# Attention scores of the first batch element as plain float32 products, 64 rows deep, in a three-layer kernel

## The chip, the cores and the metric

The kernel runs on one core of one Trainium2 chip. The metric is the time of one execution on the device in microseconds (us), as the median of several runs. A profile of one execution comes with it: each engine's instructions with start, length and what they waited for. The engines are TensorE (PE in the profile, its weight loads are PEld), VectorE (DVE), ScalarE (ACT), GpSimd (POOL) and SyncE (SP, which here issues all transfers).

## What is computed

Three layers follow one another: an attention that is causal by blocks of 64 positions, and two mixtures. Only the scores of the attention change here.

```python
B, H, S, D = 4, 8, 576, 64
scores = scale * np.matmul(q, k.transpose(0, 1, 3, 2))       # scale = 1/8
scores = np.where(block_i >= block_j, scores, -1e9)          # blocks of 64 positions
scores = scores - np.max(scores, axis=-1, keepdims=True)
attn = np.exp(scores)
attn = attn / (np.sum(attn, axis=-1, keepdims=True) + 1e-09)
x = np.matmul(attn, v)                                       # -> (2304, 512)
h = np.maximum(np.maximum(x @ w1, x @ w2), x @ w3) @ w_out   # first mixture, 512 -> 768 -> 512
# second mixture: 4 experts, each max(h @ w1[e], 0) @ w2[e], weighted by domain_probs
```

Everything is float32 in and out.

## The kernel before

**Pairs of heads.** The 8 heads of a batch element are worked on as 4 pairs; `g < NPAIR` in `load_pair` and `prep_pair` means a pair of batch element 0 (called batch 0 below), and in `scores`, `turn_probs` and `values` the number `g` counts heads, so that `g < H` means batch 0. Batch 0 takes its products of probabilities and values in plain float32 (`values32`, L310 to L322); the later batches split them in two parts.

**Scores by a split.** TensorE multiplies the type `F32R` with one pass and less precision than float32. So the kernel splits each operand in a rounded high part and the remainder. The host lays q and k out so that the 64 rows of a head stand twice, one below the other (128 rows). `keys` rounds both copies on ScalarE (L85; VectorE for pair 0) and replaces the lower one by the remainder (L122, VectorE): `kk` holds the high part in rows 0 to 63 and the low part in rows 64 to 127. `queries` makes `q1` (scaled by -1/8 and rounded, ScalarE, L133) and `q2` (the remainder, VectorE, L135). One product of `q1` with `kk` and one of `q2` with `kk`, each 128 rows deep, add up to the full score (L190). Pairs 0 and 2 (and later even ones) have their results in tiles `q1`, `q2`, `kk`, pairs 1 and 3 in `spare`, a tile that the first mixture needs only later.

**Blocks of queries.** A head has four blocks of 128 queries (`i` 0 to 3, against 128, 256, 384 and 512 keys), and the last 64 queries of both heads of a pair share one block of 128 (`i == 4`, 576 keys): zero columns beside the tails of `q1` and `q2` keep the heads apart, which takes four products. After each block but the last, `corner` (128 rows, bf16, 64 columns, L195) pushes the masked corner out of the way. VectorE takes the minimum of each block (L208), ScalarE the exponential with its sum (L215), VectorE the reciprocal of the sum (L223, L224), GpSimd the division (L226), TensorE turns the result over (L264), VectorE and ScalarE copy it to `eh` (L273, L289), and TensorE multiplies with the values.

**Order.** The program is written head by head, with the scores two heads ahead of the values; a scheduler moves instructions within each engine's list when the kernel is built. Beside the attention of batch 0 runs the conversion of the first mixture's weights (`Convert`, L418 to L453), which are handed over in float64 and turned into float32 by integer work on ScalarE, VectorE and GpSimd, while two heads of batch 1 are already begun. When all four pairs of batch 0 are through, the first mixture's products start (L505) and run between the attention of the later batches. The second mixture (L858, L940, L1017) follows.

## Time and profile before

| | |
|---|---|
| median of 3 runs | 1253.38 us (1252.73 to 1253.74) |
| the profiled execution | 1249.91 us, its span 1248.1 us |
| TensorE busy over the span | 1211.2 us (97%), 7417 products |
| VectorE, ScalarE, GpSimd busy | 929.7, 517.8, 357.1 us |
| mean granted TensorE clock | 0.996 |

The profiled execution's own time stands 1.8 us above its span (from the first to the last instruction), and 3.5 us below the median. A page of the profile gives busy time per engine, the span in slices, the chain of work that ended last, and groups of instructions; the trace behind it can be asked for any stretch, line or engine. Matmuls overlap in the records, so that the start of one and the start of the next tell its price better than its own length.

### The profile page before, as it was taken

What the parts mean: (1) busy time and instruction counts of PE and PEld (TensorE: products, weight loads), DVE (VectorE), ACT (ScalarE), POOL (GpSimd) and SP (SyncE); (2) the same over time, 40 slices, a digit from 0 to 9 for tenths busy, and PEclk for the clock granted to TensorE, in tenths of its full rate; (3) what the DMA queues carried; (4) which work ended last, traced back from release to release, by engine and by line L of the source; (5) the groups of instructions that cost most, each with busy time, mean ns of one, the idle gap of its engine ahead of it and who ended that gap; (6) DMA issues with size and microseconds to landing.
All of it is one profiled execution on the core that took longest, in us unless ns stands there. A gap on an engine that the chain in (4) does not pass through costs nothing.

```text
span 1248.1 us, 19730 instructions
## 1 busy us (share of the span) xinstructions
PE 1211.2 (97%) x7417; PEld 1157.8 (93%) x7417; DVE 929.7 (74%) x1716; ACT 517.8 (41%) x1076; POOL 357.1 (29%) x444
## 2 busy tenths in 40 slices
PE   7879998999999999999999999999999999999998
PEld 5669997999999999989999998999999999999998
DVE  7978988666565634377888896758787888686896
ACT  7977767544544421233444441233232223322222
POOL 3957786454344212243333341000000000000000
PEclk9999999999999999999999999999999999999999
DMA  8745574554533488478887864778888887776754
GB/s 304 248 164 197 170 265 161 172 153 155 183 102 119 120 287 304 150 303 332 312 311 296 310 247 162 287 274 316 300 306 311 315 314 281 253 258 228 253 210 170
DMA packets 82644, 299.69 MB, mean 240 GB/s; under 512 B 8748, under 2 KB 18036, under 8 KB 69492
## 3 DMA queue, kind: packets, MB, share of 16 engines
q1 hardware_dynamic: 82548, 298.42, 67.3%
q8 instruction: 59, 0.97, 0.3%
q14 instruction: 37, 0.30, 0.1%
HBM read 215.26 MB, written 83.14 MB: 239 GB/s over the span
## 4 chain that ended last, share of the span: by engine, by line
PE 74%; DVE 10%; DMA 5%; POOL 4%; ACT 3%; issue 3%; SPq 0%; DVEq 0%; ACTq 0%; POOLq 0%
PE m L858 24%; PE m L505 19%; PE o L1017 17%; PE st L190 3%; PE pv L359 2%; PE o L940 2%; PE o L943 2%; PE o L944 2%; DMA t<-in_e_w 2%; PE m L1017 2%; POOL p L226 2%; PE tt L264 2%; DVE mn L208 2%; DMA part<-in_e_w 1%; POOL arena L443 1%
## 5 line engine op out<-in xcount | busy, mean ns | idle before, releaser
L505 PE MATMUL m<-xh,wt 128*128 128x288 f32 x1120 | 238.4, 298 | 0.7 <-ACT mt L541 0.4
L858 PE MATMUL m<-t,w 128*128 128x384 f32 x1152 | 228.5, 336 | 0.0
L1017 PE MATMUL o<-hx,w 128*128 128x384 f32 x1176 | 225.7, 337 | 0.0
L1017 PEld LDWEIGHTS o<-hx,w 128*128 128x128 f32 x1176 | 207.8, 188 | 0.1
L858 PEld LDWEIGHTS m<-t,w 128*128 128x128 f32 x1152 | 203.4, 188 | 2.5 <-DVE tmp L878 0.4
L505 PEld LDWEIGHTS m<-xh,wt 128*128 128x128 f32 x1120 | 183.7, 188 | 1.6 <-DVE mt L543 0.8
L858 PE MATMUL m<-b,w 128*128 128x384 f32 x864 | 175.7, 337 | 2.0 <-ACT tmp L883 2.0
L505 PE MATMUL m<-xl,wt 128*128 128x288 f32 x560 | 165.3, 295 | 0.0
L858 PEld LDWEIGHTS m<-b,w 128*128 128x128 f32 x864 | 153.2, 188 | 5.1 <-ACT tmp L883 2.3
L226 POOL TENSOR_SCALAR p<-p,sm 128x128 f32<-128x128 f32 (+1 forms) x144 | 98.7, 702 | 52.1 <-DVE sm L223 17.0
L505 PEld LDWEIGHTS m<-xl,wt 128*128 128x128 f32 x560 | 105.3, 188 | 0.3
L878 DVE TENSOR_TENSOR tmp<-m,tmp 128x384 f32<-128x384 f32 x144 | 77.9, 550 | 19.4 <-PE m L858 19.2
L505 PE MATMUL m<-hh,wo 128*128 128x288 f32 x384 | 81.3, 299 | 2.9 <-ACT arena L554 1.3
L215 ACT ACTIVATE p<-st,mn 128x128 f32<-128x128 f32 (+3 forms) x144 | 78.5, 555 | 8.2 <-DVE mn L208 6.3
L988 ACT CAST hx<-hq 128x768 fp32r<-128x768 f32 x49 | 40.6, 837 | 99.0 <-PE o L1017 75.9
L190 PE MATMUL st<-kk,q 128*128 128x128 f32 (+4 forms) x336 | 71.2, 340 | 8.7 <-ACT q L133 5.5
L940 PE MATMUL o<-w,hh 128*128 128x512 f32 x192 | 74.7, 391 | 0.9 <-ACT hh L918 0.6
L813 POOL TENSOR_TENSOR w<-part,w 128x512 fp32r<-128x512 f32 x32 | 49.2, 1557 | 91.3 <-ACT w L811 61.2
L943 PE MATMUL o<-w,hh 128*128 128x512 f32 x192 | 74.7, 390 | 0.0
L944 PE MATMUL o<-w,hl 128*128 128x512 f32 x192 | 74.1, 390 | 0.0
L543 DVE TENSOR_TENSOR mt<-m,mt 128x288 f32<-128x288 f32 x96 | 43.2, 452 | 40.3 <-PE m L505 39.9
L264 PE MATMUL tt<-ident,p 128*128 128x128 f32 x400 | 61.0, 278 | 9.8 <-POOL p L226 5.4
(169 smaller groups left out, 2173.8 us busy)
## 6 DMA issues: line engine op xcount, KB each, us to landing
w<-kb SPq DMA_DIRECT2D x55, 1024.0 KB, 6.1
w<-ka SPq DMA_DIRECT2D x30, 1792.0 KB, 7.9
ka<-w SPq DMA_DIRECT2D x16, 1792.0 KB, 6.7
wt<-held SPq DMA_DIRECT2D x54, 512.0 KB, 4.1
kb<-part SPq DMA_DIRECT2D x16, 1024.0 KB, 7.0
kb<-w SPq DMA_DIRECT2D x16, 768.0 KB, 4.7
arena<-in_w SPq DMA_DIRECT2D x18, 512.0 KB, 4.0
wo<-held SPq DMA_DIRECT2D x12, 768.0 KB, 4.5
```

Source lines behind the costliest of these rows:

```text
L190: nc.tensor.matmul(out=st[:, o + c:o + c + n], lhsT=pair[part][:, q0:q0 + P], rhs=pair["kk"][:, x, c:c + n], start=m == 0, stop=m == len(t ...
L215: nc.scalar.activation(x, st[:, o:o + w], ACTF.Exp, bias=mn[:, col:col + 1], scale=-1.0, accum_out=sm[:, col:col + 1],)
L226: nc.gpsimd.tensor_scalar(x, x, sm[:, col:col + 1], 1.0, op0=ALU.mult, op1=ALU.mult)
L264: nc.tensor.transpose(tt[:, c:c + P], pt[i][:, k0:k0 + P], ident)
L505: nc.tensor.matmul(out=out_, lhsT=w, rhs=x, start=m == 0, stop=m == n - 1)
L813: eng.tensor_tensor(w[:, a:b, 1], raw[:, a:b], f(w[:, a:b, 0]), op=ALU.subtract)
L858: ins = nc.tensor.matmul(out=m, lhsT=a, rhs=b, start=start and n == 0, stop=stop and n == 3 * KH - 1, skip_group_check=True,)
L878: nc.vector.tensor_tensor(t, x, y, op=ALU.add)
L940: ins = nc.tensor.matmul(out=o, lhsT=hh[:, ts], rhs=wh, start=i == 0, stop=False)
L943: nc.tensor.matmul(out=o, lhsT=hh[:, ts], rhs=wl, start=False, stop=False)
L944: nc.tensor.matmul(out=o, lhsT=hl[:, ts], rhs=wh, start=False, stop=i == G - 1)
L1017: nc.tensor.matmul(out=o, lhsT=a, rhs=b, start=start and m == 0, stop=stop and m == 2, skip_group_check=True,)
```

## The change

For pairs of batch 0 nothing is split. The host adds an input `qk` in which a pair's k and q stand once, head 0 in rows 0 to 63 and head 1 in rows 64 to 127; a pair takes one transfer of 576 KB (pair 0: two of 288 KB) where it took two of 576 KB (pair 0: four of 288 KB). The four pairs land in two tiles that the first mixture takes later (`hh`, `hl`; the name is `plain`), so all four loads can be issued at once. The preparation is three instructions: q's first 512 queries are scaled by -1/8 in place, and the last 64 queries of the two heads are scaled into the corners of `last`, a block of 128 by 128 whose other two corners were set to zero. VectorE does that for pair 0, GpSimd for pairs 1 to 3. A block's score is then one product in float32 (type F32) over the 64 rows of its head, and the shared last block one product over all 128 rows, block-diagonal. `last` has two places, so pairs 2 and 3 write where pairs 0 and 1 were read. Later batches keep the split.

```diff
@@ -89,14 +89,23 @@
     def load_pair(g):
         b, h0 = divmod(2 * g, H)
 
-        if g % 2:
-            raw = ap_.tile([P, 2, 2, S], F32, name="raw", tag="raw")[:]
+        if g < NPAIR:
+            if g == 0:
+                pairs["hh"] = mp.tile([P, 3, 2, S], F32, name="plain", tag="hh")
+                pairs["hl"] = mp.tile([P, NF, S], F32, name="plain", tag="hl")
+                for n in range(2):
+                    nc.gpsimd.memset(pairs["hl"][:, 2 + n, 0:P].bitcast(U32), 0)
+            raw = pairs["hh"][:, g] if g < 3 else pairs["hl"][:, 0:2]
+            for n in ((0, 1), (1, 2)) if g == 0 else ((0, 2),):
+                nc.sync.dma_start(out=raw[:, n[0]:n[1]], in_=qk[g, :, n[0]:n[1]])
         else:
-            o = (B - 1) * KD * S
-            raw = arena[:, o:o + 4 * S].rearrange("p (n h s) -> p n h s", n=2, h=2)
-        for hs in ((0, 1), (1, 2)) if g == 0 else ((0, 2),):
+            if g % 2:
+                raw = ap_.tile([P, 2, 2, S], F32, name="raw", tag="raw")[:]
+            else:
+                o = (B - 1) * KD * S
+                raw = arena[:, o:o + 4 * S].rearrange("p (n h s) -> p n h s", n=2, h=2)
             for n, src in ((1, k), (0, q)):
-                nc.sync.dma_start(out=raw[:, n, hs[0]:hs[1]], in_=src[b, h0 // 2, :, hs[0]:hs[1]])
+                nc.sync.dma_start(out=raw[:, n], in_=src[b, h0 // 2])
 
         vraw = ap_.tile([P, 5, 2, D], F32, name="vraw", tag="vraw", bufs=4)
         nc.sync.dma_start(out=vraw, in_=v[b, h0 // 2])
@@ -106,19 +115,25 @@
 
 
         raw, vraw = pairs[g]["raw"], pairs[g]["vraw"]
-        if g < NPAIR and g % 2:
-
-            spare = mp.tile([P, 2 * QW + 2 * S], F32R, name="spare", tag="hh")
-            q1, q2 = spare[:, 0:QW], spare[:, QW:2 * QW]
-            kk = spare[:, 2 * QW:].rearrange("x (h s) -> x h s", h=2)
-        else:
-            q1, q2 = (ap_.tile([P, QW], F32R, name=x, tag=x, bufs=1)[:] for x in ("q1", "q2"))
-            kk = ap_.tile([P, 2, S], F32R, name="kk", tag="kk", bufs=1)[:]
+        if g < NPAIR:
+            engine = nc.gpsimd if g else nc.vector
+            last = pairs["hl"][:, 2 + g % 2, 0:P]
+            x = raw[:, 1]
+            engine.tensor_scalar(x[:, 0:S - 64], x[:, 0:S - 64], -scale, 0.0, op0=ALU.mult, op1=ALU.add)
+            for half, at in ((lo, 0), (hi, 64)):
+                engine.tensor_scalar(
+                    last[half, at:at + 64], x[half, S - 64:S], -scale, 0.0, op0=ALU.mult, op1=ALU.add
+                )
+            pairs[g].update(k=raw[:, 0], q=x, last=last)
+            yield
+            return
+        q1, q2 = (ap_.tile([P, QW], F32R, name=x, tag=x, bufs=1)[:] for x in ("q1", "q2"))
+        kk = ap_.tile([P, 2, S], F32R, name="kk", tag="kk", bufs=1)[:]
         for x in (q1, q2):
             nc.gpsimd.memset(x[:, QT + 64:QT + 128].bitcast(U32), 0)
 
         def keys(hs):
-            (rounded if g else lambda _, to, x: rounded(nc.vector, to, x))(nc.scalar, kk[:, hs], raw[:, 1, hs])
+            rounded(nc.scalar, kk[:, hs], raw[:, 1, hs])
             nc.vector.tensor_tensor(kk[hi, hs], raw[hi, 1, hs], f(kk[hi, hs]), op=ALU.subtract)
 
         def queries(hs):
@@ -134,18 +149,10 @@
             for high, low, src in zip(*parts, srcs):
                 nc.vector.scalar_tensor_tensor(low, src, -scale, f(high), op0=ALU.mult, op1=ALU.subtract)
 
-        if g == 0:
-            for h in range(2):
-                keys(slice(h, h + 1))
-                queries(slice(h, h + 1))
-            yield
-        else:
-            keys(slice(0, 2))
-            yield
-            queries(slice(0, 2))
+        keys(slice(0, 2))
+        yield
+        queries(slice(0, 2))
         pairs[g].update(q1=q1, q2=q2, kk=kk)
-        if g < NPAIR:
-            return
         vs = ap_.tile([P, 2, 5, P], F32R, name="vs", tag="vs", bufs=2)
         vh = vs[:, :, :, 0:64]
         src = vraw.rearrange("p j h d -> p h j d")
@@ -177,19 +184,25 @@
             sets.append((st, plan))
             for i, o, w in plan:
 
-                if i == 4:
-                    todo = [(QT + 64 * x, x) for x in range(2)]
+                if g < H:
+                    own = both if i == 4 else hi if h else lo
+                    terms = [(pair["last"] if i == 4 else pair["q"][own, P * i:P * i + P], pair["k"][own])]
+                elif i == 4:
+                    terms = [
+                        (pair[part][:, QT + 64 * x:QT + 64 * x + P], pair["kk"][:, x])
+                        for x in range(2) for part in ("q1", "q2")
+                    ]
                 else:
-                    todo = [(h * QT // 2 + P * i, h)]
+                    q0 = h * QT // 2 + P * i
+                    terms = [(pair[part][:, q0:q0 + P], pair["kk"][:, h]) for part in ("q1", "q2")]
                 c = 0
                 while c < w:
                     n = min(w - c, 512 - (o + c) % 512)
-                    terms = [(part, q0, x) for q0, x in todo for part in ("q1", "q2")]
                     ends = masked and i < 4 and c + n == w
-                    for m, (part, q0, x) in enumerate(terms):
+                    for m, (qs, ks) in enumerate(terms):
                         nc.tensor.matmul(
-                            out=st[:, o + c:o + c + n], lhsT=pair[part][:, q0:q0 + P],
-                            rhs=pair["kk"][:, x, c:c + n], start=m == 0, stop=m == len(terms) - 1 and not ends,
+                            out=st[:, o + c:o + c + n], lhsT=qs, rhs=ks[:, c:c + n],
+                            start=m == 0, stop=m == len(terms) - 1 and not ends,
                         )
                     if ends:
                         nc.tensor.matmul(
@@ -1301,6 +1314,8 @@
     for name in ("q", "k"):
         x = inputs[name].reshape(B, H // 2, 2, S, D).transpose(0, 1, 4, 2, 3)
         laid[name] = np.concatenate((x, x), axis=2)
+    x = np.stack([inputs[name][0].reshape(H // 2, 2, S, D) for name in ("k", "q")])
+    laid["qk"] = x.transpose(1, 2, 4, 0, 3).reshape(H // 2, P, 2, S)
     x = np.zeros((B, H // 2, 5 * P, 2, D), np.float32)
     x[:, :, 0:512] = inputs["v"][:, :, 0:512].reshape(B, H // 2, 2, 512, D).transpose(0, 1, 3, 2, 4)
     x[:, :, 5 * P - (S - 512):] = inputs["v"][:, :, 512:].reshape(B, H // 2, 2, S - 512, D).transpose(0, 1, 3, 2, 4)
```

Lines behind the scores have new numbers: L190 is L203, L195 is L208, L208 is L221, L215 is L228, L226 is L239, L264 is L277, L289 is L302, L318 is L331, L505 is L518.

The scheduler sets each engine's order anew. On VectorE, where pair 3 was prepared before (`spare`, around the first pair's probabilities being copied):

```order
L452 TENSOR_TENSOR wt<-arena,wt 128x512
L122 TENSOR_TENSOR spare<-raw,spare 64x1152
L135 SCALAR_TENSOR_TENSOR spare<-raw,spare 128x1024
L135 SCALAR_TENSOR_TENSOR spare<-raw,spare 128x2x64
L223 TENSOR_SCALAR sm<-sm 128x3
L224 RECIPROCAL sm<-sm 128x3
L289 COPY eh<-tt 128x512
L208 TENSOR_REDUCE mn<-st 128x1 x4
```

The same place now:

```order
L465 TENSOR_TENSOR wt<-arena,wt 128x512
L236 TENSOR_SCALAR sm<-sm 128x3
L237 RECIPROCAL sm<-sm 128x3
L302 COPY eh<-tt 128x512
L465 TENSOR_TENSOR wt<-arena,wt 128x512
L221 TENSOR_REDUCE mn<-st 128x1 x4
```

The three instructions of the split are gone, and nothing of the new preparation stands in their place. On ScalarE, the exponentials of the first two heads (`p`, `st` the scores, `mn` the minimum) before:

```order
L215 ACTIVATE p_167,sm<-st,mn 128x128
L215 ACTIVATE p_169,sm<-st,mn 128x384
L85 CAST spare<-raw 128x1152
L215 ACTIVATE p_172,sm<-st,mn 128x512
L215 ACTIVATE p_179,sm<-st,mn 128x256
L133 ACTIVATE spare<-raw 128x1024
L133 ACTIVATE spare<-raw 128x2x64
L215 ACTIVATE p_218,sm<-st,mn 128x128
L215 ACTIVATE p_220,sm<-st,mn 128x384
L215 ACTIVATE p_239,sm<-st,mn 128x576
```

and now:

```order
L228 ACTIVATE p_149,sm<-st,mn 128x128
L228 ACTIVATE p_151,sm<-st,mn 128x384
L228 ACTIVATE p_154,sm<-st,mn 128x512
L228 ACTIVATE p_160,sm<-st,mn 128x256
L228 ACTIVATE p_188,sm<-st,mn 128x128
L228 ACTIVATE p_190,sm<-st,mn 128x384
L85 CAST kk<-arena 128x1152
L148 ACTIVATE q_558<-arena 128x1024
L148 ACTIVATE q_558<-arena 128x2x64
L228 ACTIVATE p_202,sm<-st,mn 128x576
```

Pair 1's split is gone from between them, and the split of pair 4 (the first of batch 1), whose loads no longer wait for a place, has moved ahead of the second head's last exponentials. On GpSimd, the first head's divisions (`p`, `sm`) and the conversion (`arena`) before:

```order
L118 MEMSET q_313 128x64
L226 TENSOR_SCALAR p_167<-p_167,sm 128x128
L226 TENSOR_SCALAR p_169<-p_169,sm 128x384
L226 TENSOR_SCALAR p_172<-p_172,sm 128x512
L226 TENSOR_SCALAR p_179<-p_179,sm 128x256
L436 TENSOR_SCALAR arena<-arena 128x512
L226 TENSOR_SCALAR p_239<-p_239,sm 128x576
```

and now:

```order
L122 TENSOR_SCALAR plain<-plain 128x512
L124 TENSOR_SCALAR plain<-plain 64x64 x2
L122 TENSOR_SCALAR plain<-plain 128x512
L239 TENSOR_SCALAR p_149<-p_149,sm 128x128
L239 TENSOR_SCALAR p_151<-p_151,sm 128x384
L239 TENSOR_SCALAR p_154<-p_154,sm 128x512
L239 TENSOR_SCALAR p_160<-p_160,sm 128x256
L122 TENSOR_SCALAR plain<-plain 128x512
L124 TENSOR_SCALAR plain<-plain 64x64 x4
L449 TENSOR_SCALAR arena<-arena 128x512
L239 TENSOR_SCALAR p_202<-p_202,sm 128x576
```

Scaling stands ahead of and behind the first head's divisions, and the four small ones of pairs 2 and 3 stand ahead of the second head's. From about the first product of the first mixture on (L505), every engine's list is the same as before: the last 7074 of the 7439 instructions in TensorE's list, 1568 of VectorE's 1718, 781 of ScalarE's 934, 359 of GpSimd's 449 and 357 of SyncE's 405 stand in the same order.

## Rows read from the trace of the kernel before

**Rows 1.** Busy time of each engine by stretch (us; instructions in brackets).

```profile
core 0: us, PE busy (x) PEld busy (x) DVE busy (x) ACT busy (x) POOL busy (x), PEclk, DMA share, GB/s
21.00:56.00 35.00, 30.43 (x175) 22.66 (x174) 34.34 (x66) 31.76 (x86) 29.18 (x35) 0.95 0.70 239
56.00:89.00 33.00, 25.60 (x145) 18.55 (x144) 23.79 (x51) 26.89 (x73) 23.54 (x31) 0.95 0.56 194
0.00:89.00 89.00, 69.23 (x373) 52.25 (x374) 71.98 (x144) 72.89 (x190) 58.84 (x86) 0.94 0.70 247
89.00:520.00 431.00, 421.68 (x3116) 410.30 (x3115) 284.77 (x681) 218.55 (x531) 204.37 (x294) 1.00 0.55 180
520.00:1248.00 728.00, 720.26 (x3933) 695.29 (x3931) 572.90 (x894) 226.34 (x357) 93.94 (x64) 1.00 0.75 275
```

**Rows 2.** TensorE's waits: who for whom, us in total, times, longest.

```profile
PE st L190 <- ACT q L133: 5.5, 1, 5.5
PE tt L264 <- POOL p L226: 5.4, 2, 4.3
PE st L190 <- ACT p L215: 2.6, 2, 2.3
```

**Rows 3.** The chain that ended last, in order of time: start, us, what.

```profile
11.41 1.35 DVE spare L122
...
19.96 1.50 DVE kk L122
...
31.03 2.33 DVE spare L122
33.39 1.59 DVE spare L135 x2
```

**Rows 4.** TensorE in order of time at full clock: start, us, what.

```profile
60.13 0.44 PE L190 MATMUL st<-spare 128*128 128x128 f32 x2
60.41 0.20 PE L195 MATMUL st<-corner 128*128 128x64 bf16 x1
60.45 0.59 PE L190 MATMUL st<-spare 128*128 128x384 f32 x2
...
61.51 1.54 PE L190 MATMUL st<-kk,q 128*128 128x320 f32 x10
...
62.94 0.47 PE L310 MATMUL pv<-eh,vraw 128*128 128x128 f32 x2
63.24 2.96 PE L318 MATMUL pv<-eh,vraw 128*128 128x512 f32 x8
66.03 0.38 PE L322 MATMUL pv<-eh,vraw 128*128 128x128 f32 x2
```

**Rows 5.** Weight loads of the scores (min/median/max ns; first 30 us, all); a late stretch.

```profile
L190 PEld LDWEIGHTS st<-kk,q x24: 287/333/353, 5.5 to 12.9; 128*128 128x128 f32 x24
L190 PEld LDWEIGHTS st<-kk,q x336: 186/191/353, 5.5 to 397.7; 128*128 128x128 f32 x168
...
81.87 4.66 PE L318 MATMUL pv<-eh,vraw 128*128 128x512 f32 x8
```

**Rows 6.** The split: L87, L122, L135 before 40 us; groups of ScalarE, then GpSimd.

```profile
0.00:40.00 40.00, 0.92 (x2) 1.04 (x1) 0.96 0.81 297
0.00:40.00 40.00, 6.69 (x5) 0.96 0.81 297
0.00:40.00 40.00, 6.30 (x10) 0.96 0.81 297
...
L133 ACT ACTIVATE q<-arena 128x512 fp32r<-128x512 f32 (+3 forms) x6 | 2.8, 515 | 4.3 <-DMA arena<-in_q 4.3
L133 ACT ACTIVATE spare<-raw 128x1024 fp32r<-128x1024 f32 (+1 forms) x4 | 2.5, 683 | 0.0
L85 ACT CAST spare<-raw 128x1152 fp32r<-128x1152 f32 x2 | 2.3, 1148 | 0.0
L85 ACT CAST kk<-arena 128x1152 fp32r<-128x1152 f32 x1 | 1.2, 1157 | 0.0
L436 POOL TENSOR_SCALAR arena<-arena 128x512 f32<-128x512 f32 x9 | 6.5, 723 | 3.5 <-ACT arena L429 2.8
```

More of the change, by code (lines that the diff above doesn't have):

```diff
@@ L22, with program @@
 MOST = (1.875 - 2.0 ** -23) * 2.0 ** 32
-def program(tc, q, k, v, w123, w_out, probs, e_w1, e_w2, out):
+def program(tc, qk, q, k, v, w123, w_out, probs, e_w1, e_w2, out):
     nc = tc.nc
@@ L1324 @@
     arrays, args = {}, []
-    for name in ("q", "k", "v", "w123", "w_out", "probs", "e_w1", "e_w2"):
+    for name in ("qk", "q", "k", "v", "w123", "w_out", "probs", "e_w1", "e_w2"):
         a = np.ascontiguousarray(laid[name])
```

## The prediction

> **What bounds the kernel now.** I read busy time by stretch first, then TensorE's waits, then the chain of waits, and last single rows of TensorE's timeline. The stretches [rows 1] cut the program in three. From 89 us on, where the first mixture's products begin, TensorE is busy 421.7 of 431 us and then 720.3 of 728 us: the engine is the bound there, and nothing of the change lies there, since every engine's list is the same from about that point. Before 89 us it is busy 69.2 of 89, so 19.8 us are idle. The question is by how much the first 89 us shrink or grow; the rest then comes as much earlier or later.
>
> In that first stage several engines share the bound. Between 21 and 56 us VectorE is busy 34.3 of 35 us (98%), ScalarE 91%, TensorE 87%, GpSimd 83%; between 56 and 89 us none is over 82% [rows 1], and work goes from engine to engine. TensorE's waits by name [rows 2]: 5.5 us until the first split is there, 5.4 us for GpSimd's divisions (one of 4.3 us), 2.6 us for exponentials (one of 2.3 us). The chain of waits [rows 3] has four pieces of the split on VectorE between 11 and 35 us, 1.35 + 1.50 + 2.33 + 1.59 = 6.8 us in sum.
>
> TensorE's work at full clock in this stage: the mean granted clock of 0.94 over 89 us [rows 1] is a loss of 5.3 us, of which 0.05 x 35 = 1.75 us lie between 21 and 56 us, 0.05 x 33 = 1.65 us behind that (a late group of eight products with values lasts 4.66 us, where the same eight last 2.96 us at full clock [rows 4, 5]), and 1.9 us ahead of it. From 5.5 to some 13 us the column reads 1.00 but weight loads take 333 ns at the median, against 191 ns over all [rows 5]; I read that as the lower of the two levels, 1.2 instead of 2.4 GHz, half of 8 us lost. So 69.2 - 5.3 - 4 = 59.9 us are work.
>
> **TensorE, what is added.** Before, one head's three blocks of 128, 384 and 512 keys take 60.13 to 61.51 = 1.38 us with their corners, and the shared last block with a block of 256 takes 61.51 to 62.94 = 1.43 us [rows 4]. The other head's 256 keys I put at 0.37 us, a little above the 0.32 us of 128 keys. A pair: 2 x 1.38 + 1.43 + 0.37 = 4.56 us. After, a pair has 2 x 1280 + 576 = 3136 columns of plain float32. The nearest rows are the plain products with values, 128 rows deep: 512 + 512 + 384 + 256 = 1664 columns in 63.24 to 66.03 = 2.79 us, 1.68 ns a column [rows 4]. That is 5.27 us; 128 columns alone take 0.30 us there and not 0.215, which adds 0.17 us for two; eight corners at 0.04 us (60.41 to 60.45) add 0.32. In sum 5.76 us, so 1.2 us more a pair and 4.8 us more for four. No row shows a product 64 rows deep. Half the price would take 2 x 1280 x 0.84 ns x 4 = 8.6 us off and make TensorE's share a gain of 3.8 us; I take the full price, since a pass goes by columns in every row here; a price above it is the third rival. The Trainium skill, TensorE: Matmul & The Clock Gate, in the table of "Why this matters for your kernels", says that one product of few rows takes as long as a full one; no run here shows it yet, and by it the sum would be the one I take, not the 8.6 us less.
>
> **VectorE, ScalarE, GpSimd.** VectorE loses the split of pairs 0 to 3: 0.92 + 6.69 + 6.30 = 13.9 us [rows 6] (the 1.04 us of GpSimd in the first of these rows is another tile's). It gains pair 0's scaling, under 0.46 us for 512 columns by the 576-column row and two pieces of 64. ScalarE loses 2.8 + 2.5 + 2.3 + 1.2 = 8.8 us. GpSimd gains three scalings of 512 columns at 0.72 us [rows 6] and six small ones, which I bound by 0.25 us each: 3.7 us at most, less some small fills. The fill between 21 and 56 us would then be lower on VectorE by its largest pieces, and GpSimd's divisions run less often beside VectorE's long reads. TensorE and GpSimd are the next ones in line.
>
> **Transfers and moved work.** Batch 0's q and k come once: 2.4 MB less of the 11.9 MB of the first 40 us (297 GB/s, the last column of the first three in [rows 6]). The first two loads keep their size, and the first product waits for one scaling instead of two instructions: I leave the start at 5.5 us. Pair 4's split stands ahead of the second head's last exponentials on ScalarE. Its q is the last of 4 x 0.59 + 4 x 0.33 + 2 x 0.59 = 4.9 MB; at 297 GB/s it lands at some 16 us. What is queued behind it there are those exponentials, and TensorE waits for the room that they free. I cost that at nothing: at the lower clock pair 0's scores alone last to 5.5 + 2 x 5.76 = 17 us. If the clock rises early, that cover is gone and up to 2 us are lost, no more than the clock gave. On GpSimd the small scalings of pairs 2 and 3 wait for TensorE's last-block products of pairs 0 and 1; behind them stand a piece of the conversion and the second head's divisions, for which TensorE's turning waits. Also at nothing, with 2.3 us as the other end, the length of the wait that the start loses.
>
> **The sum.** Idle behind the start is 19.8 - 5.5 = 14.3 us: 2.3 us for the exponentials, 35 - 30.4 = 4.6 us from 21 to 56 us, 33 - 25.6 = 7.4 us from 56 to 89 us. The first went by way of ScalarE, which had pair 1's split between the exponentials, and I let it go. Of the second I let 3 us go, because VectorE, full there, loses more than that from its chain [rows 3]. Of the third I let 1 us go. That leaves 8.0 us. Of the clock's loss I keep the first 4 us, the last 1.65, and half of 1.75, 6.5 us; the loss ahead of 21 us followed the wait that goes. Together 5.5 + (59.9 + 4.8) + 6.5 + 8.0 = 84.7 us instead of 89.0: 4.3 us earlier. The profiled execution would go from 1249.9 us (span 1248.1) to 1245.6 (span 1243.8). The median of the runs lies 3.5 us above the profiled one, so 1253.4 becomes 1249.1 us.
>
> **Rivals.** *It goes dense.* With VectorE and ScalarE some 10 us lighter, TensorE waits for 4 us only and loses nothing to the clock but the first 4 us: 5.5 + 64.7 + 4 + 4 = 78.2 us, 10.8 us less, 1242.6 us. For it speaks the 98% on VectorE; against it that from 56 us on no engine is full and TensorE waits all the same.
>
> *GpSimd takes its place.* The largest named wait is for its divisions, 5.4 us [rows 2], its busy time grows, and it was at 83% where VectorE was at 98%. If waits fall only to 12 us, 5.5 + 64.7 + 6.5 + 12 = 88.7 us, within 0.3 us of before: 1253.1 us. That is also where it ends if the freed time is only filled by TensorE's own 4.8 us.
>
> *Each change of depth costs.* 32 products are 64 rows deep, each followed by a corner 128 rows deep and preceded by something 128 rows deep: 64 changes. Products overlap now: a corner lasts 0.20 us, and the next product starts 0.04 us after it [rows 4]. If TensorE must finish one before it begins one of the other depth, 0.16 us are added at each, 10.2 us in all: 84.7 + 10.2 = 94.9 us, 5.9 us slower, 1259.3 us. It beats the gain from 4.3 / 64 = 0.07 us a change on. The trace speaks neither way, since every product in it is 128 rows deep. The Trainium skill, TensorEngine Tiling (Array Packing), Tiling Modes, says that a change of tiling mode drains TensorE; by that rule this rival would be the forecast, and no row of before can show it. I don't follow it, since it gives no price and a drain of 0.05 us would leave a gain.
>
> **How the numbers follow.** Forecast 0.47, dense 0.12, GpSimd 0.26, change of depth 0.15. A measurement of this kernel can tell 0.2% (2.5 us) from no change; the forecast, at 4.3 us, leaves little to the wrong side of that, so faster 0.58, same 0.27, slower 0.15. The range reaches from the dense case, 1242 us, to a part of the third rival, 1256.5 us (0.1 us a change: 84.7 + 6.4 = 91.1 us, 1255.5 us); it leaves out most of that rival and little below.
>
> **What would show it.** The first product of the first mixture starts at about 84.7 us; before that, products with plain operands at 1.68 ns a column, with corners 0.04 us apart; VectorE's busy time there some 59 us, ScalarE's 64, GpSimd's 61; the stretches behind keep their lengths of 431 and 728 us. A gap beside the corners would speak for the third rival, waits for the divisions for the second. Wrong would be the whole sum if the stage ends earlier and the end does not, since I let all of it through.

## The result: 0.8% slower

Four runs of the kernel after have a median of 1262.49 us (1262.21 to 1264.95); four of the kernel before, beside them, 1253.06 us (1250.26 to 1253.74). The ratio is 1.0084, with a 95% interval of 1.0064 to 1.0104. The forecast was 1249.1 us, with a range from 1242 to 1256.5: the sign was wrong, and the time lies outside the range.

The profiled execution of after took 1262.21 us, its span is 1260.1. These are the stretches that answer to [rows 1], in the same columns:

```profile
21.00:56.00 35.00, 34.68 (x132) 19.93 (x130) 21.73 (x45) 21.74 (x62) 18.35 (x25) 1.00 0.36 119
56.00:97.00 41.00, 37.99 (x197) 25.24 (x197) 32.16 (x70) 34.29 (x94) 34.72 (x42) 1.00 0.55 193
0.00:97.00 97.00, 87.74 (x358) 51.91 (x359) 60.65 (x130) 64.07 (x174) 59.27 (x90) 1.00 0.56 200
97.00:528.00 431.00, 420.91 (x3106) 409.01 (x3106) 284.87 (x678) 218.80 (x532) 203.62 (x294) 1.00 0.55 180
```

Between 21 and 56 us VectorE fell from 34.34 to 21.73 us and TensorE rose from 30.43 to 34.68 of 35: TensorE is the bound of the first stage now. The first mixture product starts at 96.81 us instead of 89.00, 7.8 us later. The stretch behind is nearly as long as before: from the first of the first mixture's products to the last 431.3 us (96.8 to 528.1), before 429.9 us (89.0 to 518.9). The spans differ by more, 12.0 us, in part because the profiled execution of before (1249.91 us) lies 3.2 us under the median of its runs. From the first mixture product to the end it takes 1159.1 us, the one of after 1163.3; in e1, e3 and e10 below it is 1161.5 to 1164.7. So what has to be explained is the 7.8 us; the medians differ by 9.4 us, and the rest is not explained here.

TensorE's waits in these 97 us, answering to [rows 2]:

```profile
PE st L203 <- DVE plain L122: 5.9, 1, 5.9
PE pv L331 <- ACT eh L302: 1.0, 1, 1.0
...
PE tt L277 <- POOL p L239: 0.4, 1, 0.4
```

The 5.4 us for the divisions are 0.4 now, and the wait for exponentials ahead of the scores is 0.3 us instead of 2.6. What took their place is TensorE itself. Its rows answering to [rows 4], once early and once late (L203 the scores, L208 the corners, L331 products with values, L277 transposes):

```profile
6.83 1.64 PE L203 MATMUL st<-plain 64*128 64x384 f32 x2
8.40 0.24 PE L208 MATMUL st<-corner 128*128 128x64 bf16 x1
...
20.13 1.95 PE L277 MATMUL tt<-ident,p 128*128 128x128 f32 x8
...
31.22 4.15 PE L331 MATMUL pv<-eh,vraw 128*128 128x384 f32 x8
35.20 0.71 PE L277 MATMUL tt<-ident,p 128*128 128x128 f32 x5
...
38.21 0.20 PE L208 MATMUL st<-corner 128*128 128x64 bf16 x1
38.34 0.91 PE L203 MATMUL st<-plain 64*128 64x384 f32 x2
39.18 0.20 PE L208 MATMUL st<-corner 128*128 128x64 bf16 x1
39.31 1.12 PE L203 MATMUL st<-plain 64*128 64x512 f32 x2
40.37 0.20 PE L208 MATMUL st<-corner 128*128 128x64 bf16 x1
40.41 1.84 PE L203 MATMUL st<-plain 128*128 128x320 f32 x6
```

Two things are to be seen. First, **the clock**: a block of 384 keys lasts 1.57 us until its corner at 6.83 us (8.40 - 6.83) and 0.84 us at 38.34; eight transposes 1.95 us at 20.13 and 1.04 us late (62.53). TensorE is at the lower level, 1.2 GHz, from its first product at 5.93 us to about 35.1 us, the end of the eight products with values (31.22 to 35.20 = 3.98 us; at full clock such a group takes 2.03, 50.99 to 53.02). In before it was there until some 13 us and, behind a wait of 2.3 us, again from 17.2 to 20.5 us, where the column of the granted clock shows 0.50. In after's 29 us it is hardly idle, and half of them, some 14.5 us, are lost. The column reads 1.00 all the while, as at the start of before; that it is the clock all the same is read from the lengths, and from e4 below, where the same block takes as long under a column of 0.50. Second, **the changes of depth**: behind a corner, which is 128 rows deep, the next 64-row product starts 0.13 us later (38.21 to 38.34), the next 128-row product 0.04 us later (40.37 to 40.41).

TensorE's weight loads, in order of time, show where the second stands. In after:

```profile
38.34 0.29 PEld L203 LDWEIGHTS st<-plain 64*128 64x128 f32 x2
39.18 0.10 PEld L208 LDWEIGHTS <-corner 128*128 128x128 bf16 x1 [0.55 <-issue]
39.31 0.29 PEld L203 LDWEIGHTS st<-plain 64*128 64x128 f32 x2
```

The corner's weights are loaded at 39.18 us, when the block ends, though TensorE's loader had nothing to do for 0.55 us. In the kernel with only 128-row products (the padded one, below) the corresponding load stands 0.32 us ahead of its product at 32.12, and 0.43 us ahead of the one at 33.09:

```profile
31.80 0.10 PEld L203 LDWEIGHTS <-corner 128*128 128x128 bf16 x1
32.12 0.30 PEld L198 LDWEIGHTS st<-plain 128*128 128x128 f32 x2 [0.23 <-issue]
32.66 0.10 PEld L203 LDWEIGHTS <-corner 128*128 128x128 bf16 x1 [0.24 <-issue]
```

And in before, where a corner's load starts no earlier than its product at 60.41 us, the next product still starts 0.04 us behind the corner:

```profile
60.40 0.10 PEld L195 LDWEIGHTS <-corner 128*128 128x128 bf16 x1
```

So at a change of depth the load waits for the running product. Whether the time lost is that of the load, 0.10 us, or that of the engine running empty ahead of it, these rows don't separate. The Trainium skill, TensorEngine Tiling (Array Packing), Tiling Modes, says that a change of tiling mode drains TensorE; the trace agrees, at about 0.1 us each.

### The profile page after: what moved, and what is told of

The parts are those of the page before. It is cut to its first block, busy times and chain, and to the rows that moved or that the text cites. A ratio compares the mean times of both kernels' runs of the same rounds, so it can differ in the third digit from the quotient of the medians.

```text
span 1260.1 us, 19653 instructions
## 1 busy us (share of the span) xinstructions
PE 1231.8 (98%) x7401; PEld 1158.5 (92%) x7401; DVE 920.5 (73%) x1702; ACT 509.5 (40%) x1063; POOL 356.7 (28%) x447
## 4 chain that ended last, share of the span: by engine, by line
PE 78%; DVE 9%; DMA 5%; POOL 3%; ACT 3%; issue 2%; SPq 0%; DVEq 0%; ACTq 0%; POOLq 0%
PE m L871 24%; PE m L518 18%; PE o L1030 16%; PE st L203 5%; PE o L953 3%; PE o L956 3%; PE o L957 2%; PE pv L372 2%; PE tt L277 2%; PE m L1030 2%; DVE mn L221 2%; POOL p L239 1%; DMA kb<-part 1%; DMA part<-in_e_w 1%; DMA wo<-held 1%
## 5 line engine op out<-in xcount | busy, mean ns | idle before, releaser
L518 PE MATMUL m<-xh,wt 128*128 128x288 f32 x1120 | 238.4, 298 | 0.7 <-ACT mt L554 0.4
L518 PEld LDWEIGHTS m<-xh,wt 128*128 128x128 f32 x1120 | 183.6, 188 | 1.7 <-DVE mt L556 0.8
L518 PE MATMUL m<-xl,wt 128*128 128x288 f32 x560 | 165.4, 295 | 0.1
L239 POOL TENSOR_SCALAR p<-p,sm 128x128 f32<-128x128 f32 (+1 forms) x144 | 96.9, 691 | 55.6 <-DVE sm L237 23.1
L518 PEld LDWEIGHTS m<-xl,wt 128*128 128x128 f32 x560 | 105.2, 188 | 0.6 <-DVE xl L537 0.3
L518 PE MATMUL m<-hh,wo 128*128 128x288 f32 x384 | 81.5, 299 | 3.6 <-ACT arena L567 1.3
L228 ACT ACTIVATE p<-st,mn 128x128 f32<-128x128 f32 (+3 forms) x144 | 78.5, 553 | 14.2 <-DVE mn L221 12.1
L221 DVE TENSOR_REDUCE mn<-st 128x1 f32<-128x128 f32 (+3 forms) x144 | 66.7, 504 | 19.5 <-PE st L208 19.2
L518 PEld LDWEIGHTS m<-hh,wo 128*128 128x128 f32 x384 | 62.7, 188 | 5.8 <-ACT arena L567 1.5
```

Source lines behind the costliest of these rows:

```text
L221: nc.vector.tensor_reduce(mn[:, col:col + 1], st[:, o:o + w], axis=AX.X, op=ALU.min)
L228: nc.scalar.activation(x, st[:, o:o + w], ACTF.Exp, bias=mn[:, col:col + 1], scale=-1.0, accum_out=sm[:, col:col + 1],)
L239: nc.gpsimd.tensor_scalar(x, x, sm[:, col:col + 1], 1.0, op0=ALU.mult, op1=ALU.mult)
L518: nc.tensor.matmul(out=out_, lhsT=w, rhs=x, start=m == 0, stop=m == n - 1)
```

## The experiments

The theory after these rows: the 64-row products cost twice, by the changes of depth and by a clock that comes up late. Its rivals: plain float32 keeps the clock down whatever its depth; the gaps at the changes keep it down; a 64-row product is dear in itself. "First" is the start of the first mixture product, "low until" the time to which TensorE's rows show the lower level at the start (in some it comes back behind a wait); every ratio is to the runs of before beside it, with its 95% interval.

| kernel | blocks, corners (rows) | first, us | low until, us | median, us | ratio |
|---|---|---|---|---|---|
| before | 128, 128 | 89.0 | 13 | 1253.06 | |
| after | 64, 128 | 96.8 | 35.1 | 1262.49 | 1.0084 (1.0064 to 1.0104) |
| e1_deep128 | 128, 128 | 86.5 | 11.3 | 1250.56 | 0.9986 (0.9975 to 0.9997) |
| e2_corner64 | 64, 64 | 89.8 | 25 | 1255.55 | 1.0020 (1.0011 to 1.0029) |
| e5_blocks128_corner64 | 128, 64 | 92.2 | 16.7 | 1256.58 | 1.0025 (1.0013 to 1.0037) |
| e3_padded | 128, 128 | 82.1 | 9.3 | 1248.27 | 0.9964 (0.9950 to 0.9979) |
| e8_late64 | pair 0 at 128, pairs 1 to 3 at 64; 128 | 86.0 | 10.5 | 1250.18 | 0.9979 (0.9969 to 0.9988) |
| e9_early64 | pair 0 at 64, pairs 1 to 3 at 128; 128 | 88.9 | 23.2 | 1258.60 | 1.0044 (1.0027 to 1.0060) |
| e12_side_by_side | 64, 64, heads in turn | 98.9 | 11, and again later | 1263.66 | 1.0086 (1.0056 to 1.0116) |

"First" and "low until" come from one execution of each kernel, whose time can lie some us from the median: in e8 it is the slowest of ten (1251.57 us), in e11 the fastest (1253.55 us).

### The four pairings of depths

`e1_deep128`: all products of batch 0 at 128 rows.

```diff
-                    own = both if i == 4 else hi if h else lo
+                    own = both
```

> The kernel after, with one edit: every score product of batch 0 takes all 128 rows of its operands instead of the 64 of its head, so a block's scores sum both heads of the pair, and the output is another one; sizes, columns and counts of the work are those of the kernel after. The depth theory: what costs is the 64-row product and the change between the depths (32 blocks at about 0.29 us), and the late rise of the clock (some 15 us lost until 36 us) comes with it. Then blocks take 1.68 ns a column, the next block starts 0.04 us after a corner, and the first mixture product, at 96.8 us in the kernel after, starts between 80 and 88 us, so the run ends 9 to 16 us ahead of the kernel after, at about 1246 to 1253 us. The plain-float32 theory: the clock stays down with plain float32 of any depth, and only the 9 us of the blocks go at most, less where they lie in the first 36 us; the first mixture product at 90 to 94 us. If depth plays no part: 96 to 97 us.

`e2_corner64`: the corners at 64 rows too.

```diff
+    nc.gpsimd.memset(corner[64:65, 0:64], 1e15)
...
+                rows = (hi if h else lo) if g < H else both
...
-                            out=st[:, o + w - 64:o + w], lhsT=corner, rhs=corner[:, 0:64], start=False, stop=True
+                            out=st[:, o + w - 64:o + w], lhsT=corner[rows], rhs=corner[rows, 0:64],
```

> The kernel after, with the corner products of batch 0 also 64 rows deep (a 65th row of the corner matrix is set, so that the same sum is formed). The products stay 64 rows deep, but a block and its corner now have the same depth: of 64 changes of depth about 32 or fewer are left. If the change itself costs (0.15 us each), a block and corner lose about 0.15 us and the first mixture product comes 4 to 6 us earlier than 96.8 us, at about 91 to 93 us. If a 64-row product is dearer in itself, or its weight load isn't hidden, nothing changes: 96 to 97.5 us.

`e5_blocks128_corner64`: e1's line, with `corner[lo]` for batch 0.

> The run with all score products 128 rows deep, with the corner products now 64 rows deep: the fourth of the four pairings of depths. As there, a block's scores sum both heads, so the output is another one. The 64 changes of depth of the kernel after are back, the 64-row blocks are not. Two theories on the clock, both agree that a change takes about 0.10 us at the full clock (a 384-key block to its corner 0.84 us in the kernel after, 0.73 where both have one depth), so a block and its corner are 0.2 us longer. Rows theory: the clock stays down where TensorE works with half its rows, so here it rises at about 11 us as in the run with all at 128 rows; first mixture product 86.5 us plus up to 6.4 us, some of it covered by waits of 8 us in that run: 88 to 92 us. Gap theory: the clock stays down because of the gaps at the changes; then the lower level lasts to about 30 us again and the first mixture product comes at 94 to 97 us.

The same two blocks, late and at full clock, in e1, then e2, then e5 (TensorE in order of time):

```profile
25.21 0.89 PE L203 MATMUL st<-plain 128*128 128x384 f32 x2
25.94 0.19 PE L208 MATMUL st<-corner 128*128 128x64 bf16 x1
25.97 1.65 PE L203 MATMUL st<-plain 128*128 128x320 f32 x6
```

```profile
31.11 0.89 PE L205 MATMUL st<-plain 64*128 64x384 f32 x2
31.84 0.19 PE L210 MATMUL st<-corner 64*128 64x64 bf16 x1
31.87 1.10 PE L205 MATMUL st<-plain 64*128 64x512 f32 x2
```

```profile
19.55 0.91 PE L204 MATMUL st<-plain 128*128 128x384 f32 x2
20.39 0.20 PE L209 MATMUL st<-corner 64*128 64x64 bf16 x1
20.52 1.67 PE L204 MATMUL st<-plain 128*128 128x320 f32 x6
```

With one depth throughout, the block takes 0.73 us at 64 rows and at 128 rows, and its successor starts 0.03 us after the corner. With two depths it is 0.84 and 0.13 us, whichever of the two has the 64 rows. A 64-row product by itself is therefore neither cheaper nor dearer; the change costs 0.10 to 0.11 us. e5 and e1 have the same list of instructions on TensorE, VectorE and ScalarE: 64 changes are worth 92.2 - 86.5 = 5.7 us, 0.09 us each. That is a net figure: TensorE is busy 8.7 us longer up to there (80.55 against 71.81 us), which holds the changes and the later rise of the clock, and waits 3.1 us less. After and e2 have the same lists as well, and differ by 96.8 - 89.8 = 7.0 us, more than the 4 to 6 us that I had expected. Part of it is another thing: where the two heads' blocks follow one another, they overlap in the records. In e2 the blocks of 256, 128 and 384 keys with their corners last from 9.24 to 11.51 us:

```profile
9.24 0.84 PE L205 MATMUL st<-plain 64*128 64x128 f32 x3
...
9.87 1.01 PE L205 MATMUL st<-plain 64*128 64x256 f32 x2
...
10.68 0.84 PE L205 MATMUL st<-plain 64*128 64x384 f32 x1
...
11.51 3.44 PE L205 MATMUL st<-plain 128*128 128x320 f32 x6
```

In e1 the same three take 1.07 + 0.64 + 1.5 = 3.2 us at the lower level, 0.9 us more; `e12_side_by_side`, below, is about this.

The clock goes mainly with the rows: low until 11 and 17 us with 128-row blocks, until 25 and 35 us with 64-row blocks. The theory on plain float32 falls with e1. The theory on gaps falls as the main cause: e2 has 27 of them and is low until 25 us, e5 has all 64 and is up at 16.7 us. That is still later than e1's 11.3, so the gaps do their part. Between kernels with equal corners the rows make 96.8 - 92.2 = 4.6 and 89.8 - 86.5 = 3.3 us; here the lists of instructions differ in places as well.

### Block-diagonal for all blocks

`e3_padded`: q of every block has its own head's 64 rows and zeros in the other 64, laid so in memory.

```diff
-                    own = both if i == 4 else hi if h else lo
-                    terms = [(pair["last"] if i == 4 else pair["q"][own, P * i:P * i + P], pair["k"][own])]
+                    q0 = QT if i == 4 else h * QT // 2 + P * i
+                    terms = [(pair["q"][:, q0:q0 + P], pair["k"])]
```

> The kernel after, with every query block of batch 0 laid out block-diagonal: its own head's 64 rows and zeros in the other 64, so that each score product is 128 rows deep and still plain float32. Loads of a pair grow from 576 to 864 KB, the scaling from 576 to 1152 columns. The depth theory: as the run with 128 rows, with blocks at 1.68 ns a column and the clock up earlier, first mixture product at 81 to 89 us, the end at 1246 to 1254 us; the start may lose 1 to 2 us to the larger loads. The plain-float32 theory: 90 to 94 us.

It is the fastest, with e10: 1248.27 us, 0.36% below before, and still without a split. Its first 82 us, in the columns of [rows 1]:

```profile
0.00:82.00 82.00, 69.75 (x356) 47.91 (x356) 60.20 (x127) 61.59 (x172) 54.68 (x77) 1.00 0.65 232
```

TensorE is busy 69.75 us, and of the 82.0 us 82.0 - 4.7 - 69.75 = 7.5 us are waits behind the start.

### What holds the clock up

`e4_warm`: after, with 40 products of the corner matrix ahead of all. `e6_padded_warm128` and `e7_padded_warm64`: the same on e3, the latter with `corner[0:64]` on both sides.

```diff
+    def warm(n):
+        t = ps_v.tile([P, 512], F32, name="warm", tag="v")
+        for _ in range(n):
+            nc.tensor.matmul(out=t[:, 0:P], lhsT=corner, rhs=corner, start=True, stop=True)
+
+    warm(40)
```

> The kernel after, with 40 products of the corner matrix with itself (128 columns, 128 rows deep, bfloat16, result unused) on TensorE ahead of the first scores, where it waits 5.9 us for operands. If the late clock is only a matter of a cold start, the clock is up by 8 to 10 us, up to 13 us are saved on TensorE, of which waits for other engines take some back: first mixture product at 85 to 92 us. If 64-row products don't hold the clock up, it falls back soon and the first mixture product stays within 2 us of 96.8 us.

> The padded kernel with 40 products of the corner matrix (128 columns, 128 rows deep, bfloat16, result unused) ahead of the first scores. In the kernel after the same 40 brought the clock up, and it fell at 9.4 us. Rows theory: here it stays up. It saves half of the 4.8 us that the padded kernel spends at the lower level after its start at 4.74 us, and loses 1.4 us to its own length (it lasts to 6.2 us): first mixture product at 80.5 to 82.5 us against 82.1, the end at 1246 to 1249 us, no difference that can be measured. If plain float32 of any depth can't hold the clock, it falls at about 9.5 us and the first mixture product is at 84 us or later.

> The same with the 40 products 64 rows deep. Rows theory: products of 64 rows don't bring the clock up, so the first 128-key block behind them takes 0.59 us to its corner, as in the padded kernel, and the lower level lasts about 5 us from there, to 10 or 11 us; first mixture product at 83 to 85.5 us. If any activity brings the clock up: that block takes 0.3 us, and the run is as the one with 128 rows.

e4 by stretches (columns as in [rows 1], the granted clock third from the right), and behind them one block of 384 keys:

```profile
7.90:8.90 1.00, 1.00 (x4) 0.20 (x3) 0.67 (x2) 0.25 (x1) 0.70 (x2) 1.00 1.03 422
...
9.40:9.60 0.20, 0.20 (x2) 0.04 (x1) 0.20 (x1) 0.20 (x1) 0.00 (x0) 0.55 1.03 412
...
28.00:29.00 1.00, 1.00 (x6) 1.00 (x6) 1.00 (x2) 0.37 (x1) 0.78 (x2) 0.50 0.00 0
29.00:30.00 1.00, 1.00 (x6) 0.67 (x5) 1.00 (x2) 0.67 (x2) 0.00 (x0) 0.55 0.00 0
```

```profile
10.62 1.65 PE L210 MATMUL st<-plain 64*128 64x384 f32 x2
12.20 0.24 PE L215 MATMUL st<-corner 128*128 128x64 bf16 x1
```

The clock is up when the first scores start, falls at 9.4 us and is at 0.50 until 29 us, with TensorE busy throughout. First is 95.3 us, the median 1260.25 us (1.0066, 1.0048 to 1.0084): the 64-row products don't hold it. Here the column shows the lower level, this time reached from above, and the block of 384 keys under it takes 1.58 us (12.20 - 10.62), as in after at the start.

In e6 and e7, TensorE's rows right behind the 40 products:

```profile
5.70 0.44 PE L205 MATMUL st<-plain 128*128 128x128 f32 x2
5.97 0.19 PE L210 MATMUL st<-corner 128*128 128x64 bf16 x1
...
11.82 0.19 PE L210 MATMUL st<-corner 128*128 128x64 bf16 x1
15.47 1.85 PE L279 MATMUL tt<-ident,p 128*128 128x128 f32 x8 [3.46 <-POOL p L241]
```

```profile
6.09 0.79 PE L205 MATMUL st<-plain 128*128 128x128 f32 x2
6.67 0.26 PE L210 MATMUL st<-corner 128*128 128x64 bf16 x1
```

After 40 products of 128 rows the first block takes 0.27 us, full clock, and the scores that follow, plain float32 at 128 rows, keep it. After 40 of 64 rows it takes 0.58 us, the lower level: they did not bring it up, though they last longer, 1.72 to 6.09 us against 1.72 to 5.70. That is the row theory without any change of depth in it. As a version e6 is no gain: first is 87.4 us, the median 1254.21 us (1.0013, 1.0001 to 1.0024). TensorE is done with the first scores at 12 us and then waits 3.46 us for the divisions, and the transposes behind that wait run at the lower level again. e7 has 87.2 us and 1252.04 us (0.9989, 0.9978 to 1.0000). Both came later than I had expected; part of it is their later start, and in e6 the clock that fell behind the wait. The rest is open.

### Where the 64 rows hurt

e3, with the rows of zeros left out for some heads: `g > 1` in e8, `g < 2` in e9. In `scores` g counts heads, and I had taken it for pairs: e8 has 64 rows in pairs 1 to 3 (24 blocks, 48 changes in its trace) and e9 in pair 0 alone (8 blocks, 15 changes), not in two pairs each with 16 blocks and 32 changes, as both expectations have it.

```diff
-                    terms = [(pair["q"][:, q0:q0 + P], pair["k"])]
+                    own = (hi if h else lo) if i < 4 and g > 1 else both
+                    terms = [(pair["q"][own, q0:q0 + P], pair["k"][own])]
```

> The padded kernel, with the products of pairs 2 and 3 taken 64 rows deep (the rows with the zeros left out, same operands, same result), pairs 0 and 1 at 128 rows. Half of the 32 blocks of 64 rows, 16, and 32 changes are back, all of them late, when the clock is up. Changes alone: 32 x 0.10 = 3.2 us, less what the waits of some 8 us take up: first mixture product at 83 to 85.5 us against 82.1. If 64 rows also bring a raised clock down here, as after the 40 products, up to 8 us more: 86 to 93 us.

> The padded kernel, with the products of pairs 0 and 1 taken 64 rows deep (same operands, same result), pairs 2 and 3 at 128 rows: the counterpart of the run with pairs 2 and 3, which moved the first mixture product from 82.1 to 86.0 us, 3.9 us for 32 changes. Rows theory: here the 64-row blocks meet a cold clock and keep it down, to 20 us or later, where the padded kernel has it up at 9.3 us: 3.9 us for the changes and 4 to 8 us for the clock, so the first mixture product is at 90 to 94 us. If the place doesn't matter: 86 us.

TensorE's first product of pair 1, in e8 and then in e9:

```profile
15.20 0.48 PE L199 MATMUL st<-plain 64*128 64x128 f32 x2
```

```profile
20.78 0.63 PE L199 MATMUL st<-plain 128*128 128x128 f32 x2
```

e8 has e3's lists on all four engines: 86.0 - 82.1 = 3.9 us for 48 changes, 0.08 us each. That too is net: TensorE is busy 5.6 us longer (75.38 against 69.83 us), at most 0.12 us a change, and waits less; the medians are only 1.9 us apart. I had expected 83 to 85.5 us for 32 changes; 86.0 is what 48 came to. The clock stays up; other products stand between the blocks by then. e9, with a third of e8's 64-row blocks, costs 6.9 us, a little less than the 8 to 12 us that I had expected from twice as many blocks. Its 15 changes are some 1.6 us at 0.105 us each; the rest goes with the lower level, which lasts until 23.2 us where e3 leaves it at 9.3. So the place matters more here than the number. The whole run is 10 us longer than e3's, so part of the cost comes later, and its list on TensorE is also another one: how much the place alone is worth is not settled by this run.

### Two tries to go further

`e10_scale_k`: the factor on k, 576 columns, instead of on the padded q, 1152. `e11_zeros_on_chip`: on top of that, the zeros are filled on the chip and a pair loads 576 KB again.

```diff
-            x = raw[:, S:3 * S]
-            for c in ((0, 512), (512, 2 * S)) if g == 0 else ((0, 2 * S),):
-                y = x[:, c[0]:c[1]]
-                engine.tensor_scalar(y, y, -scale, 0.0, op0=ALU.mult, op1=ALU.add)
-            pairs[g].update(k=raw[:, 0:S], q=x)
+            x = raw[:, 0:S]
+            engine.tensor_scalar(x, x, -scale, 0.0, op0=ALU.mult, op1=ALU.add)
+            pairs[g].update(k=x, q=raw[:, S:3 * S])
```

> The padded kernel, with the factor put on k (576 columns a pair) instead of on the padded q (1152 columns): 576 columns less for VectorE once and for GpSimd three times, 2 to 3 us of GpSimd's work in all, and pair 0's scaling no longer follows the load of q. If GpSimd's time is on the path of the first stage: first mixture product 1 to 2.5 us earlier than 82.1 us, the end at 1246 to 1247.5 us. If not: within 0.5 us of the padded kernel.

> As the run with the factor on k, and the zeros of the block-diagonal q are filled on the chip, by eight fills of 576 columns in the first microseconds, so that a pair loads 576 KB as in the kernel after, not 864 KB. At the 347 GB/s of the kernel after's first 20 us that is 3.3 us less loading by pair 3. If loads hold up the first stage: another 1 to 3 us earlier. If not, or if the fills come late for pair 0: within 0.5 us of the run with the factor on k, or up to 1.5 us later.

e10: first at 82.0 us, 1248.96 us, 0.9957 (0.9940 to 0.9973), no different from e3, as expected if GpSimd's scaling isn't on the path; the order on TensorE came out differently too. e11: first at 88.0 us, 1256.45 us, 1.0028 (1.0014 to 1.0041), 6 us later than e10 where I expected 1.5 us at most. Its clock is up at 8.5 us, earlier than in the others; then TensorE waits more:

```profile
PE tt L274 <- ACT p L225: 4.0, 3, 1.8
```

The order on TensorE came out differently here as well. Why it waits for ScalarE there was not followed up; that stays open.

### Two heads side by side

`e12_side_by_side`: e2 with the scores of a pair's two heads written block by block in turn (`order` holds the blocks of both, two at a time).

```diff
+            todo = order[:1] if order[0][0] else order[:2]
+            order = order[len(todo):]
+            for last, i, h, st, o, w, _ in todo:
+                own = both if last else hi if h else lo
...
+            for last, i, h, st, o, w, _ in todo:
+                if not last:
+                    own = hi if h else lo
+                    nc.tensor.matmul(
+                        out=st[:, o + w - 64:o + w], lhsT=corner[own], rhs=corner[own, 0:64], start=False, stop=True,
```

> In the run with corners at 64 rows, products of the two heads of a pair that follow one another overlap in the records (9.87 to 10.88 us one head's 256 keys, 9.90 to 11.52 us the other's 384): 64-row products in different halves of the rows seem to run side by side. This kernel is that one with the scores of a pair's two heads written block by block in turn, for pairs 0 and 3 at least (the scheduler pulls pairs 1 and 2 apart). Side-by-side theory: two blocks of 512 keys in turn last hardly longer than one (0.95 to 1.1 us at full clock, 1.9 to 2.2 at the lower level, not 1.9 and 3.7), pair 0's scores are through 4 to 6 us earlier than there (16.66 us), and with two halves at work the clock may come up before the 24 us of that run. Then the first mixture product is at 80 to 87 us against 89.8. If the overlap in the records is only how ends are modelled: 1.9 and 3.7 us for two such blocks, and 88 to 91 us. The changed grouping also moves exponentials and turnings, which can cost 2 us either way.

TensorE in order of time:

```profile
6.97 2.06 PE L281 MATMUL st<-plain 64*128 64x512 f32 x4
8.81 0.26 PE L288 MATMUL st<-corner 64*128 64x64 bf16 x2
...
11.76 0.20 PE L288 MATMUL st<-corner 64*128 64x64 bf16 x2
15.43 1.97 PE L359 MATMUL tt<-ident,p 128*128 128x128 f32 x8 [3.47 <-POOL p L320]
...
27.68 1.13 PE L281 MATMUL st<-plain 64*128 64x512 f32 x4
28.65 0.20 PE L288 MATMUL st<-corner 64*128 64x64 bf16 x2
```

Two blocks of 512 keys in different halves of the rows take 0.97 us together at full clock (27.68 to 28.65), where one takes 0.94 in e2; at the lower level 1.84 us. The overlap is real: half the price by rows, which I had put aside in the prediction, is to be had where the heads stand in turn and nothing of 128 rows between them. The Trainium skill, TensorEngine Tiling (Array Packing), Key Properties, says that different tiles can work in parallel; the trace agrees for the two halves of the rows. In the kernel after, the corner behind every block prevents it. The run as a whole was slower, first at 98.9 us and 1263.66 us, against my expectation: pair 0's scores are through at 12 us, then TensorE waits 3.47 us for the divisions and later 3.4 and 3.0 us for copies, and the clock is down again in between (mean of 0.76 from 20 to 40 us). With the groups arranged anew more than one thing has changed, so what a better arrangement would bring stays open.

## Why the prediction was wrong

**The failed step: the choice on the third rival.** It was worked out with the right count, 64 changes (63 in the trace, where nothing stands ahead of the first block), at 0.16 us, and given 0.15. The price is 0.10 to 0.11 us by the rows, and 0.09 and 0.08 net of shorter waits by the pairs of runs e5 and e1, e8 and e3: 5 to 7 us in all, less than the rival's 10.2, more than the gain of 4.3 us. I had bounded a change from 0 to 0.16 us and put 0 into the sum, because the trace of before has no change of depth in it. That was the hopeful end of the bounds, and no row speaks for it: their middle, 0.08 us, already lies above the 0.07 us from which, by the prediction's own sum, the rival beats the gain. The Trainium skill's rule (TensorEngine Tiling (Array Packing), Tiling Modes), which I cited and set aside for want of a price, was right.

**The second failed step: the clock's loss.** I kept 6.5 us, the first 4 as before. It was about 14.5 us, since 64-row products left TensorE at the lower level to 35 us. No rival held this. Without it, the third rival's mechanism at its real price would have given 84.7 + 6.7 = 91.4 us and some 1255.8 us, inside the range. The Trainium skill, TensorE: Matmul & The Clock Gate, Part 1, says that the lower level is the default and activity releases it; by that alone the clock should have come up sooner, and the 29 busy us of after don't agree.

**What held.** The price by columns: 64 rows cost as much as 128, as I took it (0.73 us for 384 keys in e1 and in e2), as long as no product of the other half stands beside them (e12). The Trainium skill (TensorE: Matmul & The Clock Gate, "Why this matters for your kernels"), in the sentence that I cited on few rows, says the same, and the trace agrees. A pair's scores at one depth are 2 x (0.25 + 0.76 + 0.97) + 1.51 + 0.56 = 6.0 us in e3 (blocks of 128, 384, 512, the last block with one of 256, the other 256, each with its corner), where I had 5.76: 1 us too little for four pairs. The start (5.9 against 5.5 us), the busy times to the first mixture product (VectorE 60.7, ScalarE 64.1, GpSimd 59.3 us, against some 59, 64, 61) and, to some 4 of 1160 us, the stretches behind it held.

**The waits** were put at 8.0 us. In after they are 96.8 - 5.9 - 87.5 = 3.4 us, because a slower TensorE finds its operands ready. Where TensorE isn't slowed, in e3, they are 7.5 us.

Put together with the measured terms, the sum is 5.9 (start) + 64.7 (work) + 1.0 (columns) + 6.7 (64 changes at 0.105) + 14.5 (clock) + 3.4 (waits) = 96.2 us, against 96.8. That it comes out so near is no test, since most of its terms were taken from after itself. The test is the kernels with products of one depth: the forecast of 84.7 us and 1249.1 us lies between e1 (86.5, 1250.56) and e3 (82.1, 1248.27). TensorE is busy 71.8 and 69.8 us there, where the forecast had 64.7 + 6.5 = 71.2, and waits 9.7 and 7.5 us behind the start, where it had 8.0. So the other terms came out near, and one edit, the depth (e1, whose blocks sum both heads), turned the sign back; e3 does it with the right sums.

## What to carry to other kernels

Count the places where neighbouring products on TensorE have different depths, and price each (about 0.10 us here); where no row has the price, put the middle of its bounds into the sum, not the lower end. A product of half the depth by itself saves nothing, so a block with zeros in the other rows was the better form here (e3, 0.36% below before), even with 288 KB more to load per pair; half depth pays only where products of both halves follow one another. Where a stage starts cold, read the clock from the duration of one repeated shape, not from the column of the granted clock.

## What the hardware showed that I had not expected

- TensorE, busy 14.07 of 14.1 us from 5.9 to 20 us with blocks mostly 64 rows deep, stayed at the lower level until 35 us; 40 products of 64 rows left it there where 40 of 128 rows brought it up; and 64-row blocks let a raised clock fall at 9.4 us. In e8, from 15 us on and mixed with other work, they did not.
- The column of the granted clock reads 1.00 in a cold start though blocks take twice their time (1.57 against 0.84 us); it read 0.50 only where the clock had been up before (e4 from 9.6 us on; before from 18 to 20.5 us).
- A faster start can be lost at once: in e6 the scores were done by 12 us, and behind the wait of 3.46 us for the divisions TensorE was at the lower level again.
- Plain float32 products in the two halves of the rows run side by side: 0.97 us for two blocks of 512 keys (e12).
